# A Fourier mixing layer and a gated MLP on one core: half of each form's copies compared by accumulating DMAs, stored places reused later, loads spaced, h loaded from GpSimd's queue

## The chip, the cores and the metric

The kernel runs on one NeuronCore of a Trainium2 chip. Its engines work side by side and each takes its instructions in order: TensorE (PE; PEld for its weight loads) multiplies matrices, VectorE (DVE) and ScalarE (ACT) work elementwise, GpSimd (POOL) does small things and issues DMAs, SyncE (SP) issues DMAs only. A DMA's transfer is carried out by 16 DMA engines that all queues share. The metric is the device time of one execution in microseconds (us); lower is better.

## What is computed

```python
def reference(A_x, A_dft_seq_re, A_dft_seq_im, A_dft_hid_re, A_dft_hid_im, B_x, B_w1, B_w3, B_w2, gate_w):
    x = A_x                                           # 1 x 2048 x 512, float32
    g = sigmoid((x * gate_w).sum(-1, keepdims=True))
    a = einsum("bsd,ed->bse", x, dft_hid_re)          # 512 x 512
    b = einsum("bsd,ed->bse", x, dft_hid_im)
    y = einsum("ts,bse->bte", dft_seq_re, a) - einsum("ts,bse->bte", dft_seq_im, b)   # 2048 x 2048
    h = silu(x @ w1) * (x @ w3)                       # 512 x 1376 each
    out = h @ w2                                      # 1376 x 512
    return g * y + (1 - g) * out
```

The float32 products are made as three products of float32r parts: each operand is split into a rounded part ("high", on ScalarE) and the remainder ("low", on VectorE).

## The kernel before

The work runs in stages, with TensorE going from one to the next.

**Gate phase** (up to about 205 us). For 22 items (a chunk c of 128 columns of w1 and w3, and a half of the rows of x) seven products give x·w1 and x·w3 in Strassen's manner, and silu(gate)·up goes to DRAM as `hs` (`store_h`, L298, GpSimd's queue). Weights come in as `ws` (L193) and, for the second pass over a chunk, as finished parts `wb` (L200), both on SP.

**H** (about 205 to 333 us). `HSTEPS` (L910) has 22 steps, 11 chunks for each of two halves of 1024 rows. A step m multiplies a chunk of h (`ht`) by a chunk of w2 into eight PSUM banks, three matmuls a bank, 24 in all. The chunk for step m+4 is loaded (`load_h`, L914, SP) and that for m+2 is split (`high_h`, `low_h`) during step m. In the last step of a half each bank j is scaled by 1 − g into a tile `nb` (L1042 on VectorE and L1047 on ScalarE in turn), and every second one a store of two banks to `nbsp` goes out (L1043, GpSimd's queue).

**O and E** (about 333 to 349 us). Instead of the full Fourier matrices the kernel uses their symmetries: x is folded into four forms, O1a, O1b, O2 and E2 (`make_forms`, L807; the split result is `xf`), and each is multiplied by one stored tile of the matrix (`mov`, from `rep`). The results go through `e`, `s` and `z` (L1099 on) and are split again.

**Y** (from there on). Ten units of 15 short matmuls (128 or 130 columns) multiply z by the hidden matrix `DT`; VectorE adds and subtracts (L1161), combines with g and the stored `nbsp` (L1175), and SP writes the output.

**The comparison.** The symmetries hold only if the given matrices are Fourier matrices. So every stored tile is compared with the 15 other places of the matrix that should be equal to it or its negative: `wt` holds 16 tiles of 128 x 1024 for each form, the first eight of one sign, the others of the other. `compare(kind, keep)` (L713) makes tasks: load `rep` and take the sum of its absolute values (`size_rep`); load a copy, subtract or add `rep` on VectorE (`differ`, L672), sum the absolute difference on ScalarE into a column of `acc` (`add_up`, L683). With `keep` the same `rep` also yields `mov`; without it `make_mov` (L727) loads `rep` once more. The small tables have comparisons of their own (`compare_d`, `compare_small`). `verdict` (L533) compares all columns with the sizes, and if it fails, the program goes on to a general computation (`tc.If`, L1192 on), which doesn't run here.

**The order of that work.** Tasks for ScalarE ("A") and VectorE ("D") wait in `QUEUE`. The main loops call `work(eng, us)` (L565) at fixed places: it emits as many ready tasks of that engine as fit the given cost. A task is ready when its load was issued at least `LAG` calls earlier and the tasks that it needs were issued in an earlier call. Every call ends with `load_ahead` (L553), which issues loads in order on SP while at most 26 loaded tasks are unissued and free places remain beyond `RES`. Places are 4 KB tiles in a list `F4`; `take` draws the first and `free` appends, both at the time of emission, so a place can be drawn while its last reader is still at work, and the drawer waits. The calls are: in the gate phase from item 9 on, three an item; in H, at j = 1, 3, 4 and 6 of a step (L1022 to 1035); then some in O, and two in each of the first eight units of Y. Before O, `work_until(0, n_first)` (L1050) emits what is left of the tasks up to the forms, the whole comparison of O1a and all `mov` tiles; at the ninth unit of Y, `work_until(0, n_late)` emits all the rest.

Of the kernel before, what the change touches and what calls it, by code (L numbers as in the profile page):

```python
# [30 lines left out]
def fnet_swiglu_gate_kernel(  # L31
# [497 lines left out]
    acc, rep_sum = tail[:, :80], tail[:, 80:96]  # L529
    g_raw, g_pos, g_neg = (tail[:, 96 + 16 * k : 112 + 16 * k] for k in range(3))  # L530
    flag = tail[:, 144:160]

    def verdict():  # L533


        v = acc.rearrange("p (g n) -> p g n", n=16)
        nc.vector.scalar_tensor_tensor(v, v, TOL, rep_sum[:, :5, None].to_broadcast([P, 5, 16]),
                                       op0=ALU.mult, op1=ALU.is_le)
        nc.vector.tensor_reduce(flag[:, :1], acc, axis=mybir.AxisListType.X, op=ALU.add)

    def verdict_end(ps):
        nc.tensor.matmul(ps[:1, :1], flag[:, :1], nc.const_aps.tensor(1.0, [P, 1], F32), start=True, stop=True)
        nc.vector.tensor_scalar(flag[:1, 2:3], ps[:1, :1], 80.0 * P, None, op0=ALU.is_lt)
# [8 lines left out]

    def load_ahead(n):  # L553
        for i in ORDER:
# [3 lines left out]
            if sum(k not in ISSUED for k in LOADED) >= n or len(F4) < need + temps + HELD_BACK[0] + RES[0]:  # L558
                return
            if f:  # L560
                f()
            HELD_BACK[0] += temps
            LOADED[i] = NOW[0] if f else -99

    def work(eng, us, most=9, lag=None):  # L565


        NOW[0] += 1
        lag = LAG[0] if lag is None else lag
        for i in ORDER[:LIMIT[0]]:  # L570
# [5 lines left out]
            if i not in LOADED or NOW[0] - LOADED[i] < lag or any(ISSUED.get(k, NOW[0]) >= NOW[0] for k in after):  # L576
# [10 lines left out]
    def work_until(lo, hi):  # L587
        for _ in range(200):
            if all(i in ISSUED for i in range(lo, hi)):
# [57 lines left out]
    def high_x(form):  # L647
        XF[form] = lp.tile([P, 2, 1024], F32R, tag=f"m1_{GROUPS.index(form)}", name=f"xf_{form}")
        high(XF[form][:, 0], XR[form])

    def low_x(form):
        src = XR.pop(form)
        low(XF[form][:, 0], XF[form][:, 1], src)
# [14 lines left out]
    def load_t(i, src):  # L668
        TR[i] = wide(f"t{i}")
        nc.sync.dma_start(TR[i][:, : src.shape[-1]], src)  # L670

    def differ(kind, i):  # L672
        t, r = TR[16 * GROUPS.index(kind) + i], REP[kind]
        if i < 8:
            nc.vector.tensor_sub(t, t, r)  # L675
        elif kind != "E2":
            nc.vector.tensor_add(t, t, r)  # L677
        else:
            tv, rv = halves(t), halves(r)
            nc.vector.tensor_sub(tv[:, :, 0], tv[:, :, 0], rv[:, :, 0])  # L680
            nc.vector.tensor_add(tv[:, :, 1], tv[:, :, 1], rv[:, :, 1])  # L681

    def add_up(i, n=1024):  # L683
        t = TR.pop(i)
        nc.scalar.activation(t[:, :n], t[:, :n], AF.Abs, accum_out=acc[:, i : i + 1])  # L685
# [15 lines left out]
    def low_mov(kind, held=REP):  # L701
# [3 lines left out]
        if kind == "E2":  # L705
            nc.gpsimd.memset(MV[kind][:, :, :, 257].bitcast(F32), 0.0)
            nc.gpsimd.memset(MV[kind][:, :, 1::2, 128].bitcast(F32), 0.0)
            for par in range(2):
                nc.gpsimd.tensor_scalar(MV[kind][:, :, 2 * par, 128], MV[kind][:, :, 2 * par, 0].bitcast(F32),
                                        1.0 - 2.0 * par, None, op0=ALU.mult)  # L710


    def compare(kind, keep):  # L713
# [3 lines left out]
        users = task("A", 1.2, lambda: size_rep(g, REP[kind]), (), lambda: load_rep(kind), 1, 1),  # L717
        if keep:
            h = task("A", 1.0, lambda: high_mov(kind), (*users, -1))
            users += task("D", 1.2, lambda: low_mov(kind), (h,)),  # L720
        for i in range(1, 16):
            d = task("D", 1.4 if kind == "E2" and i > 7 else 1.2, lambda i=i: differ(kind, i), (),
                     lambda i=i: load_t(16 * g + i, wt[16 * g + i]), 1)
            task("A", 1.2, lambda i=i: add_up(16 * g + i), (d,))
        task("D", 0.0, lambda: free(REP.pop(kind)), (*users, d))

    def make_mov(kind):  # L727
        h = task("A", 1.0, lambda: high_mov(kind, ONCE), (-1,), lambda: load_rep(kind, ONCE), 1)
        task("D", 1.2, lambda: low_mov(kind, ONCE), (h,))
# [7 lines left out]
    def differ_d(i):  # L737
        t, r = TR[64 + i], DH[0]
# [680 lines left out]
```

## Time and profile before

| | us |
|---|---|
| median of 3 runs | 400.15 (399.53 to 402.89) |
| the profiled execution | 400.1 |
| its span, first to last instruction | 398.0 |

| stage, us from the span's start | PE busy | DVE | ACT | DMA share | granted clock |
|---|---|---|---|---|---|
| 100 to 140 (gate phase) | 40.00 | 32.34 | 27.28 | 0.71 | 1.00 |
| 140 to 200 (gate phase) | 57.63 | 48.03 | 31.83 | 0.98 | 1.00 |
| 205 to 333 (H) | 121.49 | 104.15 | 77.51 | 0.83 | 0.99 |
| 333 to 349 (O, E) | 15.62 | 7.66 | 5.03 | 0.95 | 1.00 |
| 355 to 390 (Y) | 34.57 | 33.26 | 21.27 | 0.58 | 0.50 |

The profile is of one execution. A row "A <- B" among the waits says that engine A was idle before the instruction named until B finished; "out<-in" names the tiles that an instruction writes and reads. In the last four columns of a stretch's row stand GpSimd's busy time, the TensorE clock that was granted (1.00 is full speed), the share of time in which the 16 DMA engines were busy, and GB/s.

### The profile page before, as it was taken

Reading aid. Unit: us, or ns where it says so; the run is one execution under the profiler, and the core shown is the slowest. Engines: PE = TensorE matmul, PEld = TensorE weight load, DVE = VectorE, ACT = ScalarE, POOL = GpSimd, SP = SyncE. Lnnn points to the kernel's source line nnn. Section 1 sums busy time; section 2 is a strip of 40 time slices with the busy share of each in tenths; the row PEclk is TensorE's granted clock in tenths of the full one; section 3 lists DMA queues with packets and bytes.
Section 4 is the critical chain, followed back from the end, with each engine's and each line's share of the span. In section 5 each row is a group of like instructions: output and inputs, shape, how many; then the busy total and the mean of one; then the engine's idle time right before and its main releaser. Section 6 shows DMA issues by size and latency. Waiting matters only on the chain.

```text
span 398.0 us, 5255 instructions
## 1 busy us (share of the span) xinstructions
PE 375.5 (94%) x1750; PEld 324.7 (82%) x1750; DVE 324.9 (82%) x464; ACT 234.1 (59%) x399; POOL 52.6 (13%) x105
## 2 busy tenths in 40 slices
PE   9999999999999989999998999994999999959992
PEld 5888888888888868888787888883888889849992
DVE  4999899997788959888768788886869779189992
ACT  5867765565567748543445366242859767179440
POOL 0001122111111111111114713002000002000000
PEclk9999999999999999999999999998999999975555
DMA  7459766673278999999976699694599999975651
GB/s 294 180 214 368 266 226 249 237 291 133 82 237 280 409 404 324 342 333 416 264 301 182 215 413 378 235 310 160 196 366 415 417 410 396 362 215 178 233 184 58
DMA packets 34786, 111.18 MB, mean 279 GB/s; under 512 B 5954, under 2 KB 6211, under 8 KB 32708
## 3 DMA queue, kind: packets, MB, share of 16 engines
q1 hardware_dynamic: 28868, 86.68, 60.7%
q0 software_dynamic: 5888, 24.13, 15.1%
q8 instruction: 15, 0.25, 0.2%
q14 instruction: 15, 0.12, 0.1%
HBM read 82.48 MB, written 28.32 MB: 278 GB/s over the span
## 4 chain that ended last, share of the span: by engine, by line
PE 64%; DVE 12%; DMA 11%; issue 5%; ACT 4%; POOL 1%; SPq 0%; ACTq 0%; DVEq 0%; POOLq 0%
PE X L125 22%; PE H L125 12%; PE Z L125 10%; PE Y L125 6%; DMA nbsp<-nb 3%; DMA tail<-gs 3%; DMA ws<-w 3%; PE C L125 3%; DMA w2r<-w 3%; DVE ht L114 2%; DVE t L675 2%; DVE w2t L114 1%; PE wps L384 1%; DVE nb L1042 1%; ACT t L685 1%
## 5 line engine op out<-in xcount | busy, mean ns | idle before, releaser
L125 PE MATMUL H<-w2t,ht 128*128 128x512 f32 (+1 forms) x528 | 117.0, 384 | 6.5 <-ACT nb L1047 5.2
L125 PEld LDWEIGHTS H<-w2t,ht 128*128 128x128 f32 (+1 forms) x528 | 100.5, 191 | 23.1 <-ACT nb L1047 6.4
L125 PE MATMUL X<-xo,wb 128*128 128x512 f32 x378 | 89.1, 380 | 2.4 <-DMA wb<-wbsp 1.6
L685 ACT ACTIVATE t<-t 128x1024 f32<-128x1024 f32 (+1 forms) x68 | 67.6, 1000 | 26.0 <-DVE t L681 10.0
L125 PEld LDWEIGHTS X<-xo,wb 128*128 128x128 f32 x378 | 71.2, 189 | 13.6 <-DMA wb<-wbsp 2.0
L298 POOL DMA_DIRECT2D hs<-h x40 | 21.8, 544 | 115.9 <-DVE h L358 83.3
L114 DVE TENSOR_TENSOR ht<-hr,ht 128x1024 fp32r<-128x1024 f32 x22 | 28.2, 1280 | 10.6 <-ACT ht L111 10.5
L675 DVE TENSOR_TENSOR t<-t,rep 128x1024 f32<-128x1024 f32 x28 | 33.3, 1217 | 0.0
L125 PE MATMUL Z<-xo,wb 128*128 128x512 f32 x126 | 30.6, 379 | 0.0
L125 PE MATMUL Z<-xo,wa 128*128 128x512 f32 x126 | 30.6, 379 | 0.0
L125 PE MATMUL X<-xo,wa 128*128 128x512 f32 x126 | 30.6, 379 | 0.0
L125 PE MATMUL Y<-xo,wa 128*128 128x512 f32 x126 | 30.6, 379 | 0.0
L111 ACT ACTIVATE ht<-hr 128x1024 fp32r<-128x1024 f32 x22 | 23.1, 1050 | 12.2 <-DMA hr<-hs 10.8
L677 DVE TENSOR_TENSOR t<-t,rep 128x1024 f32<-128x1024 f32 x24 | 28.1, 1220 | 0.0
L125 PEld LDWEIGHTS X<-xo,wa 128*128 128x128 f32 x126 | 23.8, 189 | 3.4
L125 PEld LDWEIGHTS Y<-xo,wa 128*128 128x128 f32 x126 | 23.8, 189 | 3.4
L125 PEld LDWEIGHTS Z<-xo,wb 128*128 128x128 f32 x126 | 23.8, 189 | 3.4
L125 PEld LDWEIGHTS Z<-xo,wa 128*128 128x128 f32 x126 | 23.8, 189 | 3.4
L114 DVE TENSOR_TENSOR wa<-ws,wa 128x768 fp32r<-128x768 f32 (+1 forms) x22 | 19.3, 881 | 7.7 <-ACT wa L111 7.5
L111 ACT ACTIVATE wa<-ws 128x768 fp32r<-128x768 f32 (+2 forms) x21 | 17.0, 808 | 13.4 <-DMA ws<-w 8.9
L369 ACT ACTIVATE h<-X 128x512 f32<-128x512 f32 x20 | 11.9, 595 | 21.6 <-PE X L125 21.5
L349 DVE TENSOR_TENSOR u<-u,X 128x512 f32<-128x512 f32 x21 | 14.4, 686 | 11.1 <-PE X L125 9.0
(292 smaller groups left out, 536.2 us busy)
## 6 DMA issues: line engine op xcount, KB each, us to landing
t<-wt SPq DMA_DIRECT2D x60, 512.0 KB, 7.9
hr<-hs SPq DMA_DIRECT2D x22, 512.0 KB, 7.3
hs<-h POOLq DMA_DIRECT2D x40, 256.0 KB, 4.3
wbsp<-wb POOLq DMA_DIRECT2D x8, 1024.0 KB, 4.2
wb<-wbsp SPq DMA_DIRECT2D x8, 1024.0 KB, 9.7
ws<-w SPq DMA_DIRECT2D x11, 512.0 KB, 4.9
xs_B<-xt SPq DMA_DIRECT2D x8, 512.0 KB, 5.5
xr<-xw SPq DMA_DIRECT2D x8, 512.0 KB, 8.5
```

The source lines that it names most:

```text
L111: nc.scalar.activation(hi, src, AF.Copy)
L114: nc.vector.tensor_sub(lo, src, hi.bitcast(F32))
L125: nc.tensor.matmul(ps.rearrange("p (n a) -> p n a", a=2), u, turns(v)[:, some], **kw)
L298: nc.gpsimd.dma_start(hs[c][:, b * TB : (b + 1) * TB], h)
L349: nc.vector.tensor_add(u4, u4, x)
L369: nc.scalar.activation(g1, x, AF.Silu)
L384: nc.tensor.matmul(wps, warm[:, :P], warm, start=True, stop=True)
L675: nc.vector.tensor_sub(t, t, r)
L677: nc.vector.tensor_add(t, t, r)
L685: nc.scalar.activation(t[:, :n], t[:, :n], AF.Abs, accum_out=acc[:, i : i + 1])
L1042: nc.vector.tensor_scalar(to, H[j], by, None, op0=ALU.mult)
```

## The change

For O1a, O1b and O2, the eight copies of equal sign are loaded as before. From seven of them `rep` is subtracted into a second tile `a` (`apart`), which is summed. Onto each loaded copy itself, and for the last one onto `rep`, a copy of the other sign is then added by an accumulating DMA on GpSimd's queue (`opposite`), and ScalarE sums the absolute value of what is left. For E2 the tiles are laid out anew on the host (real parts first, then imaginary parts): the imaginary halves of the other sign are accumulated (`opposite_im`, 256 KB each), and four tiles with the remaining real halves have `rep`'s real half subtracted (`apart_re`). A form thus has up to 20 columns in `acc` instead of 16.

A sum that follows an accumulating DMA is marked `(d, True)`, and `passed` lets it be emitted only `LAND` calls after the task that issued the DMA (4 in the gate phase, 8 from H on). `free_later` gives the place of a stored `nb` back after `LAND` calls, not at once. `load_ahead` has tokens: `RATE` of them (0.8, from H on 0.6) come with each call, at most 1.5 are held, a load spends one for each tile and waits while the count is below zero. `RES` is 5 in the last three steps of a half and 2 otherwise. The loads of h from m = 6 on are issued on GpSimd's queue. O1b and E2 are compared with `keep`, so `rep` is loaded once for each; the tasks that must be emitted before O are now a set, `MUST` (forms, edges, `mov` tiles, `DT`), and the rest of O1a's comparison is not among them. `xf` takes two places of `F4` for each form; the pool that it lived in becomes eight further places from the gate phase on. In H's second half every other step has one more `work("A", 1.2)`.

```diff
+    def free_later(*tiles):
+        for t in tiles:
+            _, places, at = HELD.pop(id(t))
+            COLD.append((NOW[0] + LAND[0], places, at))
+
+    def thaw():
+        for c in [c for c in COLD if c[0] <= NOW[0]]:
+            COLD.remove(c)
+            c[1].append(c[2])
+
+    def passed(k):
+        k, wait = k if isinstance(k, tuple) else (k, False)
+        return k in ISSUED and ISSUED[k] + (LAND[0] if wait else 1) <= NOW[0]
+
     def load_ahead(n):
+        thaw()
         for i in ORDER:
...
+            if f and TOKENS[0] < 0:
+                return
             if f:
                 f()
+                TOKENS[0] -= need
...
+        TOKENS[0] = min(TOKENS[0] + RATE[0], 1.5)
...
-    def work_until(lo, hi):
+    def work_until(ids):
+        ORDER.sort(key=lambda i: i not in ids)
...
     def high_x(form):
-        XF[form] = lp.tile([P, 2, 1024], F32R, tag=f"m1_{GROUPS.index(form)}", name=f"xf_{form}")
-        high(XF[form][:, 0], XR[form])
+        XF[form] = [take(F4, [P, 1024], F32R, f"xf{h}_{form}") for h in range(2)]
+        high(XF[form][0], XR[form])
...
-    def differ(kind, i):
-        t, r = TR[16 * GROUPS.index(kind) + i], REP[kind]
-        if i < 8:
-            nc.vector.tensor_sub(t, t, r)
-        elif kind != "E2":
-            nc.vector.tensor_add(t, t, r)
-        else:
-            tv, rv = halves(t), halves(r)
-            nc.vector.tensor_sub(tv[:, :, 0], tv[:, :, 0], rv[:, :, 0])
-            nc.vector.tensor_add(tv[:, :, 1], tv[:, :, 1], rv[:, :, 1])
+    def apart(g, i):
+
+        t = TR[20 * g + i] = wide(f"a{g}_{i}")
+        nc.vector.tensor_sub(t, TR["up", g, i], REP[GROUPS[g]])
+
+    def opposite(g, i):
+
+        nc.gpsimd.dma_start(TR["up", g, i], wt[16 * g + 8 + i], accum_op=ALU.add)
+        TR[20 * g + 8 + i] = TR.pop(("up", g, i))
+
+    def opposite_im(g, i):
+        t = TR["up", g, i]
+        nc.gpsimd.dma_start(t[:, 512:], wt[16 * g + 12 + i // 2][:, 512 * (i % 2) : 512 * (i % 2) + 512],
+                            accum_op=ALU.add)
+        TR[20 * g + 12 + i] = TR.pop(("up", g, i))
+
+    def apart_re(g, j):
+        t, r = TR[20 * g + 8 + j], REP[GROUPS[g]]
+        tv = t.rearrange("p (k n) -> p k n", k=2)
+        nc.vector.tensor_sub(tv, tv, r[:, None, :512].to_broadcast([P, 2, 512]))
...
-        for i in range(1, 16):
-            d = task("D", 1.4 if kind == "E2" and i > 7 else 1.2, lambda i=i: differ(kind, i), (),
-                     lambda i=i: load_t(16 * g + i, wt[16 * g + i]), 1)
-            task("A", 1.2, lambda i=i: add_up(16 * g + i), (d,))
-        task("D", 0.0, lambda: free(REP.pop(kind)), (*users, d))
+        def sum_of(i, d):
+            if kind == "E2":
+                task("A", 0.7, lambda: add_up(20 * g + 12 + i, 1024, 512), ((d, True),))
+            else:
+                task("A", 1.1, lambda: add_up(20 * g + 8 + i), ((d, True),))
+
+        def part(i):
+            apart(g, i)
+            meet(i)
+
+        for i in range(1, 8):
+            d = task("D", 1.2, lambda i=i: part(i), (), lambda i=i: load_t(("up", g, i), wt[16 * g + i]), 1, 1)
+            task("A", 1.1, lambda i=i: add_up(20 * g + i), (d,))
+            sum_of(i, d)
+            users += d,
+        if kind == "E2":
+            for j in range(4):
+                d = task("D", 1.2, lambda j=j: apart_re(g, j), (),
+                         lambda j=j: load_t(20 * g + 8 + j, wt[16 * g + 8 + j]), 1)
+                task("A", 1.1, lambda j=j: add_up(20 * g + 8 + j), (d,))
+                users += d,
+
+        def last():
+            TR["up", g, 0] = REP.pop(kind)
+            meet(0)
+
+        d = task("D", 0.0, last, users)
+        sum_of(0, d)
...
     compare("O1a", True)
+    MUST.update(range(n_forms))
     make_mov("O2")
     make_d()
-    make_mov("O1b")
-    make_mov("E2")
-    n_first = len(QUEUE)
+    compare("O1b", True)
+    compare("E2", True)
     compare_small()
-    compare("O1b", False)
-    compare("E2", False)
...
-            nc.sync.dma_start(HR[m], hs[c][:, half * 1024 : (half + 1) * 1024])
+            (nc.sync if m < 6 else nc.gpsimd).dma_start(HR[m], hs[c][:, half * 1024 : (half + 1) * 1024])
...
-            F4.extend((lp, f"f4_{k}") for k in range(8, 14))
+            F4.extend((lp, f"f4_{k}") for k in range(8, 22))
...
-    LAG[0], RES[0] = 4, 2
+    LAG[0], LAND[0], RATE[0] = 4, 8, 0.6
...
+        RES[0] = 5 if i > NC - 4 else 2
...
             if j == 6:
                 work("D", 1.3)
+                if half and m % 2 and not last:
+                    work("A", 1.2)
...
-                    free(nbt)
+                    free_later(nbt)
...
-    work_until(0, n_first)
+    work_until(MUST)
```

More of the change, by code (lines that the diff above doesn't have):

```diff
@@ L528, in fnet_swiglu_gate_kernel @@
     tail = const.tile([P, 160], F32, tag="tail", name="tail")
-    acc, rep_sum = tail[:, :80], tail[:, 80:96]
-    g_raw, g_pos, g_neg = (tail[:, 96 + 16 * k : 112 + 16 * k] for k in range(3))
-    flag = tail[:, 144:160]
+    acc, rep_sum = tail[:, :100], tail[:, 100:108]
+    g_raw, g_pos, g_neg = (tail[:, 108 + 16 * k : 124 + 16 * k] for k in range(3))
+    flag = tail[:, 156:160]
     def verdict():
-        v = acc.rearrange("p (g n) -> p g n", n=16)
-        nc.vector.scalar_tensor_tensor(v, v, TOL, rep_sum[:, :5, None].to_broadcast([P, 5, 16]),
+        v = acc.rearrange("p (g n) -> p g n", n=20)
+        nc.vector.scalar_tensor_tensor(v, v, TOL, rep_sum[:, :5, None].to_broadcast([P, 5, 20]),
                                        op0=ALU.mult, op1=ALU.is_le)
@@ L575, in work @@
                 break
-            if i not in LOADED or NOW[0] - LOADED[i] < lag or any(ISSUED.get(k, NOW[0]) >= NOW[0] for k in after):
+            if i not in LOADED or NOW[0] - LOADED[i] < lag or not all(passed(k) for k in after):
                 continue
@@ L585, in fnet_swiglu_gate_kernel @@
     AHEAD = [26]
-    def work_until(lo, hi):
+    def work_until(ids):
+        ORDER.sort(key=lambda i: i not in ids)
         for _ in range(200):
-            if all(i in ISSUED for i in range(lo, hi)):
+            if all(i in ISSUED for i in ids):
                 return
@@ L989, in fnet_swiglu_gate_kernel @@
     f4d_cm, f4d = pool("f4d", 1, "right")
-    F4.extend((f4d, f"f4_{k}") for k in range(16, 23))
+    F4.extend((f4d, f"f4_{k}") for k in range(24, 31))
     w2_cm, w2p = pool("w2", 1, "right")
@@ L1182, in fnet_swiglu_gate_kernel @@
         if u == 8:
-            work_until(0, n_late)
+            work_until(set(range(n_late)))
             verdict()
```

65 lines of the change are left out of this document (41 added, 24 removed).

## The prediction, made before the change was run

> **What bounds the kernel now.** The page comes first, then who waited for whom, then the chain of waits, then stretches with their granted clock.
>
> ```profile
> span 398.0 us, 5255 instructions
> ...
> PE 375.5 (94%) x1750; PEld 324.7 (82%) x1750; DVE 324.9 (82%) x464; ACT 234.1 (59%) x399; POOL 52.6 (13%) x105
> ...
> PEclk9999999999999999999999999998999999975555
> DMA  7459766673278999999976699694599999975651
> ```
>
> TensorE is busy 94% of the span, so the kernel gets shorter only where TensorE waits, where its clock is low, or where another engine ends last. The clock row shows the second: in the last four or five slices of 10 us it is at or near half. TensorE's own waits are few (columns: total us, times, longest):
>
> ```profile
> PE H L125 <- ACT nb L1047: 5.2, 3, 3.4
> PE Y0a L125 <- ACT z_O L111: 2.7, 1, 2.7
> PE X L125 <- DMA wb<-wbsp: 1.6, 1, 1.6
> PE Y0a L125 <- ACT e L1100: 1.6, 1, 1.6
> ```
>
> The releaser is mostly ScalarE. What held ScalarE itself from 270 to 346 us:
>
> ```profile
> ACT nb L1047 <- DMA nbsp<-nb: 7.8, 2, 4.3
> ```
>
> The chain (start us, us, what) has the same stores, between the halves of H,
>
> ```profile
> 276.08 3.21 DMA nbsp<-nb
> ```
>
> and after H:
>
> ```profile
> 336.83 0.77 DVE nb L1042
> ...
> 338.99 6.20 DMA nbsp<-nb
> ...
> 345.30 0.61 ACT e L1100
> ```
>
> Each time the next step is held by the store of an evacuated bank: the place was given back when the store was issued, and the next nb (between the halves) or e0 (after H) drew that very place and had to see the store land. From here on the chain is TensorE alone, without a gap to the last unit of Y:
>
> ```profile
> 355.43 1.30 PE Y0a L125 x4
> ```
>
> ```profile
> 371.06 1.28 PE Y4b L125 x6
> 372.34 2.30 PE Y5a L125 x9
> ```
>
> The clock follows from the waits (the number behind the five engines is the granted clock, then the DMA share and GB/s):
>
> ```profile
> 275.00:276.00 1.00, 0.66 (x2) 0.57 (x3) 1.00 (x3) 0.87 (x2) 0.00 (x0) 0.76 0.00 0
> 276.00:277.00 1.00, 1.00 (x3) 0.80 (x3) 1.00 (x2) 0.00 (x0) 0.92 (x2) 0.50 0.00 0
> 278.00:279.00 1.00, 1.00 (x4) 0.82 (x3) 0.00 (x0) 0.00 (x0) 0.00 (x0) 0.53 0.86 315
> 370.00:375.00 5.00, 5.00 (x23) 4.64 (x23) 5.00 (x12) 1.43 (x3) 0.00 (x0) 0.50 0.53 183
> ```
>
> Behind the long wait between the halves it is half for 0.48 + 2 + 0.94 = 3.4 us, then full again. In Y it stays at 0.50 though TensorE is never without work.
>
> **The change, part by part.** The profiled execution took 400.1 us, 2.1 of it outside the span; the median is 400.15, so the sum is made against 400.1.
>
> *Places of stored banks reused later; five places kept back in the last three steps of a half.* This answers the waits between the halves.
>
> ```profile
> L125 PE MATMUL H<-w2t,ht 128*128 128x512 f32 (+1 forms) x528 | 117.0, 384 | 6.5 <-ACT nb L1047 5.2
> ```
>
> Matmuls of H follow one another every 117.0 / 528 = 0.222 us, so in its last step TensorE finishes a bank every 0.66 us; two engines evacuate in turn, 0.7 to 0.8 us each, so the evacuation keeps up and only the landing of the store (3.2) made it late. The 5.2 us go, and with them the half clock, which lost half of 3.4: **−6.9**. Late next is the evacuation, which keeps up: nothing.
>
> *The same after H.* TensorE goes on with O and E meanwhile and ends them here:
>
> ```profile
> 345.95 0.94 PE L125 MATMUL E_1a<-mov_E,xf_E 128*128 128x258 f32 x6 [0.38 <-ACT e L1100]
> ```
>
> ```profile
> 348.87 0.49 PE L125 MATMUL E_1b<-er_p,edge_p 1*1 1x258 f32 x3
> ```
>
> that is at 349.4, or 349.0 without its wait of 0.38. From e0 (345.3) the rest of z took until Y0a (355.43), 10.1 us. Begun when VectorE's last evacuation ends, at 337.6, it is done by 347.7, before TensorE needs it. So Y begins at 349.0 instead of 355.43; five of Y0a's nine matmuls had been done by then, at 0.21 (Y4b's 1.28 / 6) 1.1 us: 6.4 − 1.1 = **−5.3**.
>
> *Loads spaced by tokens.* This thins the bursts in the gate phase and may remove the 1.6 us that TensorE waits for wb. Bounds: 0 and −1.6; the row names a load that a burst explains, so **−1.6**.
>
> *Half of the copies by accumulating DMAs.* VectorE's part of it now:
>
> ```profile
> L677 DVE TENSOR_TENSOR t<-t,rep 128x1024 f32<-128x1024 f32 x24 | 28.1, 1220 | 0.0
> ```
>
> ```profile
> L681 DVE TENSOR_TENSOR t<-t,rep 128x512 f32<-128x512 f32 x8 | 5.6, 702 | 0.0
> L680 DVE TENSOR_TENSOR t<-t,rep 128x512 f32<-128x512 f32 x8 | 5.6, 702 | 0.0
> ```
>
> The 24 additions go, and for E2's eight pairs (11.2) come four subtractions at 1.22: 28.1 + 11.2 − 4.9 = 34.4 us less. VectorE's tasks from H on, counted in the code, fall from 66 to 46. This is off the path while TensorE leads, and counts in Y only if TensorE is faster there than VectorE (below). ScalarE sums as much as before (8 halves for 4 wholes); two repeated loads of rep fall away. The price:
>
> ```profile
> q0 software_dynamic: 5888, 24.13, 15.1%
> ```
>
> ```profile
> 205.00:333.00 128.00, 121.49 (x550) 104.38 (x550) 104.15 (x118) 77.51 (x128) 21.63 (x46) 0.99 0.83 308
> ```
>
> ```profile
> t<-wt SPq DMA_DIRECT2D x60, 512.0 KB, 7.9
> ```
>
> No accumulate is in the trace. GpSimd's queue moved 24.13 MB in 15.1% of 398 us of the 16 engines, 401 GB/s, so 512 KB take 1.31 us of all of them. The low end is that an accumulate costs what the load costs that it replaces (it brings the same bytes from the same place, so no gain); the high end is two more passes, one to read the destination and one for a write that waits for it, 2.6 us. H has 8 + 8 + half of 8 = 20 of them: 0 to 52 us of DMA time, 26 with one pass. H leaves 17% of 128 us free, 21.8, and the two reps give back 2.6: 24.4, about one pass. The nearest row is the load; I take it with part of one pass and charge nothing to the path. Landing: a sum on ScalarE is placed eight calls of work behind its accumulate, two steps of 24 matmuls, 10.7 us, against 7.9 for a load.
>
> The Trainium skill ("DMA: Bandwidth & Descriptors", Rules for kernel authors) says that an accumulating DMA reads its destination and writes it later. No run here shows it yet; an estimate from it, three movements for two, gives half a pass more, 13 us in H, still inside the cover.
>
> *Who waits behind it.* On GpSimd's queue the accumulate waits for its subtraction on VectorE; behind it stand the loads of h from the seventh on, the bank stores and the small copies of the forms. A load of h is issued almost two steps before ScalarE splits it: 0 while VectorE is less than that late, one step (5.3) each time it isn't.
>
> *h on GpSimd's queue* lifts it over comparison loads that wait for places on SP:
>
> ```profile
> SPq L918 <- ACT t L685: 15.9, 3, 10.4
> ```
>
> TensorE's largest waits name no hr, so 0.
>
> *E2's banks in another order, xf in tile places, a verdict over 100 columns* only change addresses and small widths: 0.
>
> *Y.* A unit takes TensorE 2.30 + 1.28 = 3.58 us at half clock. VectorE beside it:
>
> ```profile
> 371.65 0.77 DVE L1161 TENSOR_TENSOR w<-Y3a,w 128x258 f32<-128x258 f32 x2
> 372.32 1.68 DVE L1175 SCALAR_TENSOR_TENSOR r<-w,tail,nbr 128x256 f32<-128x256 f32 x4
> 373.90 0.70 DVE L680 TENSOR_TENSOR t<-t,rep 128x512 f32<-128x512 f32 x1
> 374.50 0.70 DVE L681 TENSOR_TENSOR t<-t,rep 128x512 f32<-128x512 f32 x1
> ```
>
> ```profile
> 382.00 0.79 DVE L1161 TENSOR_TENSOR w<-Y6a,w 128x258 f32<-128x258 f32 x2
> 382.67 0.90 DVE L1175 SCALAR_TENSOR_TENSOR r<-w,tail,nbr 128x256 f32<-128x256 f32 x2
> ```
>
> The first four rows follow each other at once, 3.45 us from one L1161 to the next, all but equal to TensorE; without comparison work it is 2.45, and 1.69 in the last four units. While the clock is half this relief is worth nothing: ten units keep 35.8 us. But Y now begins at full clock, and one period of 3.4 us at full rate before it falls is **−1.7**.
>
> Sum: −6.9 − 5.3 − 1.6 − 1.7 = −15.5, so 384.6, said as **385**.
>
> **The rivals.** *The clock holds through Y.* VectorE then sets the pace: 6 × 2.45 + 4 × 1.69 = 21.5, with 2.5 for the first unit's way to VectorE 24 instead of 35.8: 11.8 less, 1.7 of it counted already, so 384.6 − 10.1 = 374.5, **374**. For it: waits of 1.6 us left the clock full, and only the longest ones (3.4, 2.7) brought it down. Against it: 30 us of Y without a gap did not raise it, so these short matmuls weigh little, and at VectorE's pace there are fewer of them in a microsecond of TensorE's time at full clock.
>
> The Trainium skill ("TensorE: Matmul & The Clock Gate", Part 1) has full clock after one busy window of about 3.4 us and half after an idle one. The 3.4 us between the halves agree; Y, busy for 30 us at 0.50, does not. By that rule a Y that begins at full clock and never idles for a window keeps it, which is this rival.
>
> *The work reappears in Y.* Spaced loads and two places for each copy make E2's comparison late; VectorE takes two subtractions with a unit (2.4), 2.45 + 2.4 = 4.9 over TensorE's 3.58. If all 12 of E2's tasks are left, six units lose 1.3 each, 8 us, and the last accumulate with its sum (7.9 and 1) stands before the verdict; 8 + 6 or so of 15.5 are given back, **399**. For it: the pairs L680 and L681 ran there before. Against it: 20 tasks fewer.
>
> *Slower: accumulates saturate the DMA engines in H.* H's DMA time is 0.83 × 128 = 106, less 2.6, plus 26 for each extra pass. At one pass it is 129.6, about as long as H is now: the point from which it decides. At one and a half it is 142.6; h lands late behind accumulates on its own queue, ScalarE stands in order before sums that have not landed, and H takes 14.6 longer than its 128. With the 6.9 inside H swallowed and 8.6 kept, 400.1 + 14.6 − 8.6 = **406**; at two passes 419. For it: the DMA row has nines through much of H. Against it: late copies can slide into Y, where the DMA share is 0.53.
>
> **How the numbers follow.** Chances: forecast (385, own range 379 to 391) 0.40; held clock (374, 369 to 379) 0.24; work in Y (399, 394 to 404) 0.14; saturated (406, 402 to 420) 0.22. With both signs in it the range runs from 370, nearly the bottom of the held clock, to 405, which takes in one pass and leaves out most of the saturated case: some 0.03 below, 0.16 above. One per cent, 4 us, is about what a measurement can tell. Faster than 396.1: 0.40 + 0.24 = 0.64; within 1%: nearly all of the third case, 0.13; slower: the saturated one and a rest of the third, 0.23.
>
> **What would show it.** Right: no wait for nbsp on ScalarE, clock 1.00 between the halves, Y0a directly behind E_1b, units of 3.58 with the clock falling soon after Y begins, VectorE with idle time there. Held clock: units of about 2.5 and no fives in the clock row. Work in Y: subtractions of copies beside the units. Saturated: accumulates landing later than 11 us, ScalarE waiting for them and for hr, a DMA share near 1 through H. The forecast is wrong if TensorE's waits in H add up to more than 6 us.

## The result, and the profile after

The changed kernel takes 432.98 us, the median of four runs (430.88 to 435.57), beside 400.2 for the kernel before on the same chip: a ratio of 1.081, 95% interval 1.073 to 1.089. The forecast was 385, the range 370 to 405; the direction was wrong. The profiled execution took 430.9 us.

These lines are from the page of the changed kernel. In the rows of queues stand packets, MB and the share of 16 engines' span; in those of instructions, busy us, mean ns of one, and the idle time before them with what ended most of it.

```profile
span 429.0 us, 5216 instructions
...
PE 384.9 (90%) x1750; PEld 326.7 (76%) x1750; DVE 291.8 (68%) x428; ACT 234.6 (55%) x407; POOL 91.4 (21%) x153
...
PEclk9999999999999969989999999998966998899655
DMA  8469665635287999999897344589998999999761
...
q0 software_dynamic: 12800, 47.20, 37.3%
...
L125 PE MATMUL H<-w2t,ht 128*128 128x512 f32 (+1 forms) x528 | 128.7, 406 | 22.0 <-ACT ht L111 13.4
...
L111 ACT ACTIVATE ht<-hr 128x1024 fp32r<-128x1024 f32 x22 | 23.1, 1048 | 43.1 <-DMA hr<-hs 40.9
...
L703 POOL DMA_DIRECT2D up<-wt x21 | 18.1, 864 | 53.8 <-DVE a L699 26.7
```

VectorE fell from 324.9 to 291.8 us, 33.1, as the change meant it to (34.4 was predicted), and the span rose by 31.0. TensorE is busy 90% instead of 94%. The DMA row has nines from about 140 to 225 us and eights and nines from 280 to about 395, with a hollow (threes to fives) between them. H's matmuls were idle for 22.0 us, most of it for ScalarE's split of h, and ScalarE in turn stood 40.9 us for the landing of h. More than 6 us of waits in H was the forecast's own sign of being wrong. TensorE's own list of waits (total, times, longest) names the two stages that lost:

```profile
PE H L125 <- ACT ht L111: 13.4, 4, 5.8
PE X L125 <- DMA wb<-wbsp: 8.9, 2, 4.6
PE X L125 <- DVE u L349: 3.5, 3, 1.8
```

The store of nb is gone from the top of the list. The chain of waits of the changed kernel shows transfers in its place, one in the gate phase and three in H, the two longest of which stand here, and behind them Y:

```profile
143.21 22.43 DMA xr<-xw
...
314.13 9.88 DMA hr<-hs
...
357.64 10.02 DMA hr<-hs
...
391.69 1.43 PE Y0a L125 x9
...
398.98 0.72 PE Y3b L125 x6
399.70 2.31 PE Y4a L125 x9
```

Stages are best bounded by the first matmul of H and the first of O, here in the timeline of the changed kernel:

```profile
226.46 13.87 PE L125 MATMUL H<-w2t,ht 128*128 128x512 f32 x63 [1.44 <-ACT h L369]
...
376.21 0.60 PE L125 MATMUL O<-mov_O1a,xf_O1a 128*128 128x256 f32 x3 [0.52 <-ACT nb L1119]
```

The same two places read from the timelines of the kernel before and of the experiments below give this table (us):

| kernel | H begins | O begins | span | H | from O on |
|---|---|---|---|---|---|
| before | 211.0 | 333.3 | 398.0 | 122.3 | 64.7 |
| changed | 226.5 | 376.2 | 429.0 | 149.7 | 52.8 |
| before + places later (e4) | 210.7 | 327.5 | 385.8 | 116.8 | 58.3 |
| changed, second copies left out (e3) | 210.3 | 331.3 | 387.3 | 121.0 | 56.0 |
| changed, second copies loaded plainly (e2) | 217.7 | 347.3 | 402.5 | 129.6 | 55.2 |
| the same, h on SP (f3) | 218.1 | 339.8 | 396.8 | 121.7 | 57.0 |
| accumulates in the gate phase only (f1) | 226.7 | 347.6 | 404.6 | 121.0 | 57.0 |
| accumulates after the gate phase only (f2) | 210.0 | 360.7 | 417.7 | 150.7 | 57.0 |

The gate phase lost 15.5 us and H 27.4; from O on 11.9 were gained: 15.5 + 27.4 − 11.9 = 31.0, the difference of the spans. (The stage table ahead of the forecast starts H at 205 us; its first matmul is at 211.0.) The stretches of the changed kernel show what the DMA engines did meanwhile (the last three columns are the granted clock, the DMA share and GB/s):

```profile
140.00:200.00 60.00, 48.12 (x200) 40.13 (x199) 33.17 (x42) 30.11 (x54) 9.07 (x14) 0.91 1.04 354
...
220.00:275.00 55.00, 51.65 (x236) 44.05 (x235) 40.89 (x51) 27.36 (x42) 22.46 (x44) 1.00 0.56 191
275.00:371.00 96.00, 77.38 (x297) 62.15 (x297) 44.76 (x46) 49.38 (x83) 25.21 (x34) 0.88 0.96 273
```

In the gate phase and in the larger part of H the engines are full, and H's first part leaves 44% of 55 us, 24 us of them, unused.

TensorE's losses make up these sums. In H it waited 22.0 us instead of 6.5 and its matmuls took 128.7 instead of 117.0: 15.5 + 11.7 = 27.2 of the 27.4. The second term agrees with the clock: 0.88 over 96 us is worth an estimated 0.12 × 96 = 11.5 us. In the gate phase the waits for wb and u rose from 1.6 and 0.5 to 8.9 and 3.5, and the clock of 0.91 over 60 us adds an estimated 5.4: 15.7 of 15.5. In Y the clock works the other way: the first four units took 8.0 us at full clock instead of 4 × 3.58 = 14.3. With the 5.3 of the earlier start that is 11.6 of the 11.9.

### The profile page after: what moved, and what is told of

It is laid out like the page before. It is cut to its first block, busy times and chain, and to the rows that moved or that the text cites. A ratio compares the mean times of both kernels' runs of the same rounds, so it can differ in the third digit from the quotient of the medians.

```text
span 429.0 us, 5216 instructions
## 1 busy us (share of the span) xinstructions
PE 384.9 (90%) x1750; PEld 326.7 (76%) x1750; DVE 291.8 (68%) x428; ACT 234.6 (55%) x407; POOL 91.4 (21%) x153
## 3 DMA queue, kind: packets, MB, share of 16 engines
q0 software_dynamic: 12800, 47.20, 37.3%
## 4 chain that ended last, share of the span: by engine, by line
PE 42%; issue 28%; DMA 12%; POOL 9%; ACT 3%; DVE 3%; SPq 0%; POOLq 0%; ACTq 0%; DVEq 0%
PE X L125 17%; PE Z L125 8%; DMA hr<-hs 6%; DMA xr<-xw 5%; PE Y L125 5%; PE C L125 3%; PE O L125 2%; POOL up L703 2%; POOL hs L298 2%; ACT ht L111 1%; POOL edge L860 1%; DMA xs_B<-xt 1%; POOL hr L987 1%; ACT a L719 1%; POOL rep L703 1%
## 5 line engine op out<-in xcount | busy, mean ns | idle before, releaser
L125 PE MATMUL H<-w2t,ht 128*128 128x512 f32 (+1 forms) x528 | 128.7, 406 | 22.0 <-ACT ht L111 13.4
L125 PEld LDWEIGHTS H<-w2t,ht 128*128 128x128 f32 (+1 forms) x528 | 105.9, 203 | 44.7 <-ACT ht L111 15.5
L125 PE MATMUL X<-xo,wb 128*128 128x512 f32 x378 | 92.2, 389 | 12.5 <-DMA wb<-wbsp 8.9
L125 PEld LDWEIGHTS X<-xo,wb 128*128 128x128 f32 x378 | 72.5, 193 | 25.3 <-DMA wb<-wbsp 9.7
L114 DVE TENSOR_TENSOR ht<-hr,ht 128x1024 fp32r<-128x1024 f32 x22 | 27.9, 1269 | 53.1 <-ACT ht L111 53.1
L111 ACT ACTIVATE ht<-hr 128x1024 fp32r<-128x1024 f32 x22 | 23.1, 1048 | 43.1 <-DMA hr<-hs 40.9
L699 DVE TENSOR_TENSOR a<-up,rep 128x1024 f32<-128x1024 f32 x28 | 33.2, 1217 | 2.6 <-DMA up<-wt 2.6
L719 ACT ACTIVATE a<-a 128x1024 f32<-128x1024 f32 x28 | 29.3, 1046 | 6.5 <-DVE a L699 6.5
L125 PE MATMUL Z<-xo,wb 128*128 128x512 f32 x126 | 32.3, 395 | 0.0
L703 POOL DMA_DIRECT2D up<-wt x21 | 18.1, 864 | 53.8 <-DVE a L699 26.7
L719 ACT ACTIVATE up<-up 128x1024 f32<-128x1024 f32 (+1 forms) x28 | 26.3, 939 | 4.1 <-DMA up<-wt 4.1
L369 ACT ACTIVATE h<-X 128x512 f32<-128x512 f32 x20 | 11.9, 594 | 29.9 <-PE X L125 25.2
L125 PEld LDWEIGHTS Z<-xo,wb 128*128 128x128 f32 x126 | 25.1, 199 | 4.0
L349 DVE TENSOR_TENSOR u<-u,X 128x512 f32<-128x512 f32 x21 | 14.4, 684 | 20.3 <-PE X L125 15.5
```

The lines of the kernel that those rows point to most:

```text
L111: nc.scalar.activation(hi, src, AF.Copy)
L114: nc.vector.tensor_sub(lo, src, hi.bitcast(F32))
L125: nc.tensor.matmul(ps.rearrange("p (n a) -> p n a", a=2), u, turns(v)[:, some], **kw)
L349: nc.vector.tensor_add(u4, u4, x)
L369: nc.scalar.activation(g1, x, AF.Silu)
L699: nc.vector.tensor_sub(t, TR["up", g, i], REP[GROUPS[g]])
```

## The experiments

Times are medians; ratios are to the kernel before on the same chip, with 95% intervals. A difference between two experiments is taken from their ratios, times 400.15 us. Every run that leaves out a part of the comparison (e2, e3, f1, f2, f3, g1, g4, p1) also has the verdict's factor `TOL` set to 0, so that the short path is taken.

**e1: h back on SP.**

```diff
-            (nc.sync if m < 6 else nc.gpsimd).dma_start(HR[m], hs[c][:, half * 1024 : (half + 1) * 1024])
+            nc.sync.dma_start(HR[m], hs[c][:, half * 1024 : (half + 1) * 1024])
```

> The changed kernel with one part undone: all loads of h are issued on SP's queue again. Three theories. Engine time (an accumulate of 512 KB takes the 16 DMA engines about 2.8 us instead of 1.31, so they are full at 140 to 200 and 275 to 380 us and everything lands late): no byte changes, so 424 to 436. Queue order (h stands on GpSimd's queue behind accumulates, stores and their waits): TensorE's 13 to 22 us of waiting in H go, about 410. Spacing (tokens and the eight more places put the loads of x and of the copies at a bad time, whatever they are): no change, 430.

Measured: 427.46, 1.0662 [1.0638, 1.0686]. The queue accounts for 0.0147, 5.9 us; most of the loss stays when h no longer stands behind the accumulates.

**e2: plain loads in the place of the accumulating DMAs.**

```diff
-nc.gpsimd.dma_start(TR["up", g, i], wt[16 * g + 8 + i], accum_op=ALU.add)
+nc.gpsimd.dma_start(TR["up", g, i], wt[16 * g + 8 + i])
```

and the same for `opposite_im`.

> The changed kernel with the accumulating DMAs made plain loads of the same bytes into the same tiles from the same queue: copies of the other sign overwrite instead of being added, so the second half of the comparison is left out, and the verdict's factor is 0 so that the short path is taken. Engine time: the DMA time falls by 28 x 1.5 = 42 us, and the time to 395 to 402. Queue order: GpSimd's queue holds the same instructions with the same waits, so 420 to 433. Spacing: 425 to 433.

Measured: 404.51, 1.0113 [1.0078, 1.0148], a little above what the theory of engine time gave and far below what the rivals gave. The same bytes on the same queue in the same order cost 27.9 us less when nothing is added. From the page of e2, its queue and its issuing instruction:

```profile
q0 software_dynamic: 12288, 47.20, 30.5%
```

```profile
L703 POOL DMA_DIRECT2D up<-wt x21 | 11.2, 533 | 38.0 <-DVE a L699 30.5 <-ACT mov_O1b L111 3.5 <-ACT rep L718 1.0
```

**e3: the accumulating DMAs left out.**

```diff
-nc.gpsimd.dma_start(TR["up", g, i], wt[16 * g + 8 + i], accum_op=ALU.add)
```

and the same for `opposite_im`.

> The changed kernel without the accumulating DMAs (24 of 512 KB and 8 of 256 KB left out; ScalarE sums the loaded copies as they are; factor of the verdict 0). It shows what all the rest of the change is worth. Engine time: 385 to 392, where the prediction was without a price for the accumulates. Queue order: the same 385 to 392, since nothing stands before h. Spacing: 420 or more, and TensorE still waits at 150 to 180 us.

Measured: 389.07, 0.969 [0.9631, 0.975], as expected. Everything else in the change together, without the second copies, is a gain; the second copies, 28 transfers' worth of 512 KB, cost 0.1119, 44.8 us. From the page of e3:

```profile
q0 software_dynamic: 8192, 32.52, 21.9%
```

The three queue rows give the price of a transfer. GpSimd's queue took 21.9% of 387.3 = 84.8 us of all 16 engines without second copies, 30.5% of 402.5 = 122.8 with plain ones, 37.3% of 429.0 = 160.0 with accumulating ones. For the 28 × 512 KB (47.20 − 32.52 = 14.68 MB) that is 38.0 / 28 = 1.36 us for a load and 75.2 / 28 = **2.69 us for an accumulate**: twice, one whole pass more. (This puts the whole difference of the queue's time down to the 28; f1 with 8 and f2 with 20 of them, below, give 2.65 and 2.76.) It shows in the stretch of e2 that answers to the changed kernel's last:

```profile
275.00:347.00 72.00, 63.84 (x277) 53.60 (x275) 40.99 (x39) 50.34 (x86) 18.68 (x37) 0.95 0.94 361
```

At nearly the same share, 0.94 and 0.96, all transfers together move 361 GB/s with plain loads and 273 with accumulates among them.

**e4: the kernel before, with only the places reused later and kept back.**

```diff
+            COLD.append((NOW[0] + 8, places, at))
...
+        RES[0] = 5 if i > NC - 4 else 2
...
-                    free(nbt)
+                    free_later(nbt)
```

> The kernel before with one part of the change alone: places of stored banks are given back eight calls later, and five places are kept back in the last three steps of a half. If the prediction's two terms hold (-6.9 between the halves, -5.3 before Y), 388; if another wait takes the place of the one removed, 396 to 401.

Measured: 387.72, 0.9655 [0.9625, 0.9685], as the two terms gave. It is the lowest median of the study, ahead of the kernels before and after; e3's interval overlaps it. Its page and TensorE's first wait in H:

```profile
PE 371.0 (96%) x1750; PEld 322.0 (83%) x1750; DVE 324.6 (84%) x464; ACT 233.2 (60%) x399; POOL 53.4 (14%) x105
...
PEclk9999999999999999999999999999999999995555
```

```profile
PE H L125 <- ACT nb L1058: 1.2, 1, 1.2
```

TensorE is busy 96%, and the dent in the clock between the halves is gone. e3, with 33 us less of VectorE's work, isn't faster than this. But e3 also has h on GpSimd's queue, which by itself costs e4 5.7 us (h1, below), and the new order, so it doesn't show what VectorE's relief alone is worth.

**f1 and f2: accumulates only for O2 (in the gate phase), and only for the other three forms.**

```diff
-        nc.gpsimd.dma_start(TR["up", g, i], wt[16 * g + 8 + i], accum_op=ALU.add)
+        if g == 2:
+            nc.gpsimd.dma_start(TR["up", g, i], wt[16 * g + 8 + i], accum_op=ALU.add)
```

with `opposite_im`'s left out as well; f2 has `g != 2` and keeps `opposite_im`'s.

> The changed kernel with accumulating DMAs for O2 alone (8, all in the gate phase); those of O1a, O1b and E2 are left out (24 and 8 minus 8, the sums take the loaded copies as they are; verdict's factor 0). Without any it took 389.1, with all 433. Engine time: 8 x 2.7 = 21.6 us more DMA time at 140 to 200 us, where the DMA engines are full, so the gate phase's stalls come back, 10 to 16 us: 399 to 405. Queue order (the harm comes in H, by h behind accumulates): 389 to 392.

> The counterpart: accumulating DMAs for O1a, O1b and E2, none for O2 (its 8 left out, verdict's factor 0). If the two parts add up, 389 + 44 less what the run with O2 alone costs, 415 to 425 by engine time; by queue order nearly all of it, 428 to 433.

Measured: f1 406.4, 1.0151 [1.0105, 1.0198], 18.4 us over e3, a little above its range; f2 418.48, 1.0452 [1.0389, 1.0515], 30.5 over e3, inside it. The two add up to 48.9, near the 44.8 of all together. In the table above f1 begins H as late as the changed kernel and has the H of e3; f2 has it the other way round. The stretches from 140 to 200 us of f1 and of f2, in this order, show the same:

```profile
140.00:200.00 60.00, 48.77 (x200) 40.49 (x199) 33.05 (x43) 29.98 (x54) 9.09 (x14) 0.89 1.04 354
```

```profile
140.00:200.00 60.00, 59.50 (x275) 51.44 (x273) 47.50 (x65) 36.65 (x70) 7.61 (x14) 1.00 1.00 366
```

Eight accumulates in the gate phase take 11 us of TensorE's work out of that stretch of 60 us, and in f2 it is untouched.

**g1: every second copy half as wide** (the second half of every comparison's columns is not added).

```diff
-nc.gpsimd.dma_start(TR["up", g, i], wt[16 * g + 8 + i], accum_op=ALU.add)
+nc.gpsimd.dma_start(TR["up", g, i][:, :512], wt[16 * g + 8 + i][:, :512], accum_op=ALU.add)
```

> The changed kernel with every accumulating DMA at half its width (256 KB instead of 512, 128 KB for E2; the other halves left out, verdict's factor 0): the same instructions, waits and places, half the bytes. Engine time: DMA time falls by half of 75 us, and the time about as with plain loads of full width, which take half the engine time too, 398 to 406. Queue order: the instructions and what they wait for are as before, 422 to 433.

Measured: 410.33, 1.0247 [1.018, 1.0314]. With as many instructions and waits on GpSimd's queue as in the changed kernel, half the bytes cost half the time (22.3 of 44.8 us over e3). That is above the 398 to 406 of engine time and far below the 422 to 433 of queue order, which is refuted. Its queue row:

```profile
q0 software_dynamic: 12800, 39.86, 31.5%
```

Of its span of 405.0 that is 127.6, 42.8 over e3, so the price holds, 1.53 us for 256 KB.

Set side by side, the extra time of the DMA engines over e3 and what it cost (us):

| | extra DMA time | cost over e3 | hidden |
|---|---|---|---|
| f1, gate phase alone | 21.2 | 18.4 | 2.8 |
| e2, plain | 38.0 | 16.9 | 21.1 |
| g1, half width | 42.8 | 22.3 | 20.5 |
| f2, after the gate phase | 55.1 | 30.5 | 24.6 |
| changed | 75.2 | 44.8 | 30.4 |

(f1: 26.2% of 404.6; f2: 33.5% of 417.7, less 84.8 each. All costs share e3's interval, ± 2.4.) In the four rows with transfers in H 20 to 30 us are hidden, though the extra time is 38 in one and 75 in another; what lies above is paid. In the gate phase nearly nothing is hidden.

**f3: plain loads, and h on SP**: e1's edit and e2's together.

> Plain loads in place of the accumulating DMAs (the second half of the comparison left out, verdict's factor 0), and h loaded on SP's queue. With h on GpSimd's queue this took 404.5. If h behind those loads is what is left of the harm (4.2 us of TensorE waiting for h in that trace), 398 to 400; if it is the DMA time of the loads at full stretches, 403 to 406; if h behind comparison loads on SP is worse, 406 to 410.

Measured: 396.59, 0.9904 [0.9873, 0.9936], below all three expectations. h on GpSimd's queue costs 0.0209, 8.4 us, with plain loads. In the table above it is all in H: 129.6 beside 121.7.

**h1: e4 with h on GpSimd's queue**, without any second copy there.

```diff
-            nc.sync.dma_start(HR[m], hs[c][:, half * 1024 : (half + 1) * 1024])
+            (nc.sync if m < 6 else nc.gpsimd).dma_start(HR[m], hs[c][:, half * 1024 : (half + 1) * 1024])
```

> The kernel before with places reused later (387.7 alone) and, added, the loads of h from the seventh on on GpSimd's queue; no accumulates. If that move costs by itself (it took 5.5 with accumulates and 8 with plain loads in front of it), 393 to 396; if it costs only behind other loads on that queue, 386 to 390.

Measured: 392.54, 0.9797 [0.9764, 0.983], 5.7 us over e4, nearly what the move was expected to cost by itself. The waits of h1 (e4 has 13.4 in the first row):

```profile
ACT ht L111 <- DMA hr<-hs: 20.6, 4, 10.2
POOL hr L928 <- ACT t L695: 11.3, 3, 6.1
POOL hr L928 <- DMA nbsp<-nb: 4.4, 1, 4.4
```

On GpSimd a load of h meets waits that have nothing to do with accumulates: it stands for the place that ScalarE's sum gives back, and for the landing of a store of nb.

**f4: no tokens.**

```diff
-            if f and TOKENS[0] < 0:
-                return
```

> The changed kernel with the tokens off: loads go out as soon as a place and the window of 26 tasks allow it, accumulates as changed. If the spacing is what makes the loads late and bunched (H's first half has a DMA share near 0.5, its second near 1), 415 to 425; if engine time of the accumulates sets it and the tokens hardly bind, 430 to 436; if the spacing helps as its name says, 437 or more.

Measured: 430.16, 1.074 [1.0669, 1.0812]. The interval overlaps the changed kernel's; spacing the loads gained nothing that shows, and TensorE waits for wb with tokens (8.9 us) as without (5.8).

**p1: f3 with the eight places of the new xf pool joining only when H begins.**

```diff
-F4.extend((lp, f"f4_{k}") for k in range(8, 22))
+F4.extend((lp, f"f4_{k}") for k in range(8, 14))
...
+    F4.extend((lp, f"f4_{k}") for k in range(14, 22))
```

> Plain loads in place of the accumulates, h on SP (second half of the comparison left out, verdict's factor 0; 396.6 in that form), and now the eight places that xf gave up join the list only when H begins. What is left there against 389 lies at 140 to 200 us: x's forms are loaded beside the second copies of O2. If the eight places cause that (more loads in flight at once), 389 to 391; if the second copies themselves do (they can start only behind the subtraction, so they fall into the full stretch), 395 to 398.

Measured: 397.44, 0.9875 [0.9822, 0.9929], not to be told from f3. More places are not what fills the gate phase's DMA engines.

**h2: e4 with the order of the change** (rep loaded once for O1b and E2, `MUST`), without accumulates.

```diff
-    make_mov("O1b")
-    make_mov("E2")
...
+    compare("O1b", True)
+    compare("E2", True)
```

> The kernel before with places reused later and with the order of the change that needs no accumulate: O1b and E2 compared with the kept rep (two loads of 512 KB fewer) and only forms, edges, mov tiles and the hidden matrix forced before O. TensorE waits little now, so 386 to 389 if Y at half clock (ten units of 3.58) ends last as before; below 385 only if VectorE's work in Y had been ending last.

Measured: 396.43, 0.9877 [0.9828, 0.9927]: the order by itself costs e4 8.9 us, where no loss was expected. The trace, of an execution that took 403.4 us, has this as TensorE's longest wait:

```profile
PE E_0a L125 <- POOL mov_E L720: 7.7, 1, 7.7
```

In the chain of that trace the split of mov_E stands on VectorE behind ten subtractions of the comparison, and GpSimd's work on it takes 4.85 us more. How much of it the other executions have isn't shown, so the cause stays open. In the changed kernel E follows O, and Y follows E, without a gap, so that it isn't a term of its time as it stands.

**g2, g3, g4, g5: the room for the descriptors of GpSimd's DMAs.** 512 instead of 1024 bytes a partition for the changed kernel (g2), for plain loads (g4) and for the kernel before (g5), and 1152 for the changed kernel (g3).

```diff
-    nc = bacc.Bacc("TRN2", target_bir_lowering=False, num_devices=1, dynamic_dma_scratch_size=1024)
+    nc = bacc.Bacc("TRN2", target_bir_lowering=False, num_devices=1, dynamic_dma_scratch_size=512)
```

> The changed kernel with half the memory set aside for the descriptors of GpSimd's DMAs (512 bytes a partition instead of 1024), all else as changed. GpSimd stood 20 us before accumulates with nothing named as the releaser. If it was waiting for room for descriptors, that idle time at least doubles and the time goes to 437 or more; if the accumulates' time on the DMA engines alone decides, 429 to 435 and the idle time stays near 20.

> The changed kernel with 1152 instead of 1024 bytes per partition for the descriptors of GpSimd's DMAs, nothing else changed. Halving the room cost 63 us (495.7 against 433.0). If the room already delays GpSimd's issues in the changed kernel (its page shows 19.4 us of issue idle before the accumulates), an eighth more should give some of it back: 422 to 430. If at 1024 the room is just enough and the engine time of the accumulates sets the end, nothing moves: 431 to 435.

> The plain-loads kernel (second half of every comparison overwritten, not added: that half is left out of the result) with 512 instead of 1024 bytes per partition for the descriptors. It moves the same bytes on GpSimd's queue as the changed kernel. If the room counts descriptors alone, it loses as much as the changed kernel did: 460 or more from 404.5. If what counts is how long the descriptors stay in it, and plain loads stay about half as long (1.36 against 2.69 us of engine time per 512 KB), it loses less than half as much: 406 to 430.

> The kernel before with 512 instead of 1024 bytes per partition for the descriptors. Its GpSimd queue moves 24.1 MB, the changed kernel's 47. If half the room binds any kernel, it is slower by 20 us or more; if the room binds only under the traffic that the change puts on GpSimd's queue, 399 to 404.

Measured: g2 495.74, 1.2371 [1.231, 1.2432]; g3 432.92, 1.0832 [1.0776, 1.0887]; g4 412.96, 1.0287 [1.0214, 1.0359]; g5 414.04, 1.0339 [1.0292, 1.0386]. Half the room costs the changed kernel 62.5 us, the plain loads 7.0 and the kernel before 13.6 (this last between its two expectations). An eighth more gives nothing back; a larger room wasn't tried. The waits of GpSimd's instructions for nothing that the profile shows, from the changed kernel, g2 and g5 in this order:

```profile
POOL up L703 <- issue: 14.5, 7, 4.2
```

```profile
POOL up L703 <- issue: 68.4, 14, 8.3
```

```profile
POOL nbsp L1043 <- issue: 16.1, 4, 4.6
```

With half the room the issues themselves stall, of accumulates in g2 and of the stores of nb in g5 (1.7 us in the kernel before).

Summed over all second copies, GpSimd stood 23.2 us in this way in the changed kernel, 23.4 in g3, 17.6 in g1, 12.6 in e1 and 1.4 before the plain loads of e2. So GpSimd stalls before accumulates at the changed kernel's own room as well; what for isn't shown. The stall by itself doesn't explain the cost over e3: in g1 it falls by a quarter and the cost by half, in e1 it falls by nearly half and the cost by an eighth.

## Why the prediction was wrong, step by step

**The step that failed** is the price of the accumulating DMAs: "The nearest row is the load; I take it with part of one pass and charge nothing to the path." Three things were wrong with it.

The size: an accumulate takes 2.69 us of all 16 engines where a load takes 1.36, one whole pass more. The bounds (0 to 2 passes) held it, and 26 us for H's 20 is what the forecast itself gave for one pass; the value taken was too low. Yet by the forecast's own cover of 24.4 one pass would have cost 1.6 us, so that the size alone doesn't explain the loss. The Trainium skill ("DMA: Bandwidth & Descriptors", Rules for kernel authors) has an accumulate read its destination and write it later. The trace agrees with an extra movement; the estimate of three movements for two was too low, since the time doubled.

The stretch: the eight accumulates of O2 fall into the gate phase, whose share of 0.98 stood in the table of the kernel before, and the forecast summed only H's. There they have no cover: H begins 7.4 us later with plain second copies than with none, and 16.2 later with accumulating ones (210.3, 217.7, 226.5).

The cover: 24.4 us were counted as free in H, and 24 us are free in it after the change, but in its first part (share 0.56 up to 275 us), while the accumulates come in the rest (0.96). The first accumulate of H is issued at 279.4. A mean share over 128 us said nothing about when the free time lies.

**h on GpSimd's queue** was priced at 0 because TensorE's largest waits named no hr. ScalarE's list of the kernel before did:

```profile
ACT ht L111 <- DMA hr<-hs: 10.8, 5, 4.1
```

It costs 5.7 us on e4, 5.9 in the changed kernel and 8.4 with plain loads. The row against SP's queue that the forecast quoted (15.9 us behind places) was answered by waits of the same kind on GpSimd.

**Who waits behind the accumulate**: bounds of 0 or 5.3 for each load of h, 0 taken. ScalarE stood 40.9 us for h in the changed kernel, and TensorE 13.4 for ScalarE's split. With h on SP (e1) these fall to 15.3 and 8.9, and H from 149.7 to 141.5 (229.1 to 370.5). So the queue is 8.2 us of it, and the rest, 20.5 over e3's 121.0, stays when h isn't behind the accumulates.

**Places reused later, between the halves and after H** (−6.9 and −5.3) held, with the −1.7 for Y's first period: together 13.9, measured in e4 13.8 [12.6, 15.0]. In the traces H gains 5.5, as 2.1 us of waits for the evacuation stay where none was forecast, and the rest from O on gains 6.4. In the changed kernel, too, no wait for nbsp is left and Y0a follows E_1b at once.

**The tokens** (−1.6) failed: the wait for wb rose from 1.6 to 8.9 us, and taking the tokens away moved nothing that can be told. In e3, with tokens and without second copies, TensorE has no wait for wb; in f1, with the gate phase's accumulates alone, it has 9.3. So the accumulates brought the wait back.

**VectorE's relief** was right in size (33.1 of 34.4). Its worth was taken as nothing, which agrees with Y's last six units, each a period of TensorE at half clock without a gap; no run changes VectorE's work alone, so it isn't shown by itself.

**The rivals.** The held clock is refuted: units of 3.58 us (2.30 and 1.28) from the fifth on. But the four units before them are 6.3 us shorter together than at half clock, where the forecast had 1.7. The work reappearing in Y wasn't seen: from O on the changed kernel is 11.9 us shorter than the kernel before. The saturated DMA engines are what happened. The rival's price for H, 14.6 us at one and a half passes, came out as 27.4 at one pass, for h's queue (7.9 by e2 against f3, 8.2 by the changed kernel against e1) and the unused first part of H lie on top; and it left the gate phase out altogether. Its evidence, the nines in the DMA row and a point of decision at one pass, was on the table.

The way from 400.15 to 433, by ratios: places reused later −13.8; the rest of the order with plain second copies, h on SP, +10.0 (e4 to f3; 7.5 of it is H's later begin); h on GpSimd's queue +8.4; the adding itself +27.9. That is 32.5 of the 32.4 us lost. What else in the order makes up the 10.0 besides the later second copies in the gate phase stays open.

## What to carry to other kernels

An accumulating DMA of this kind (128 x 1024 float32, from DRAM onto a tile) takes work from VectorE only to give twice a load's time to the DMA engines: cost it as two transfers, and do so stage by stage, against the share of the stage in which it falls. Where TensorE is made to wait, look at the granted clock too: in H the longer matmuls cost 11.7 us beside 15.5 of waits. A mean share over a long stage is no cover; look at shorter stretches for where the free time lies. And a load that a compute engine waits for shouldn't be moved behind instructions with waits of their own on another queue, even when its wait isn't on TensorE's list.

## What the runs showed of the hardware that was not expected

An accumulating DMA costs 2.69 us of all 16 engines per 512 KB beside 1.36 for a plain one, and its issue occupies GpSimd for 864 ns beside 533. GpSimd's issues stall when the room for their descriptors is short, and accumulates stall far more than loads: half the room cost 62.5 us with them and 7.0 with plain loads of the same bytes. Bytes alone don't order the loss: the kernel before, with half of them on that queue, lost 13.6.

The clock in Y falls without any idle time before it: the first four units of the changed kernel ran at full clock, about 2.0 us each from 391.69 on, and at 399.70, without a gap, the units became 3.58 us long and stayed so. The Trainium skill ("TensorE: Matmul & The Clock Gate", Part 1) lowers the clock after an idle window; this trace doesn't agree, as it fell after 8 us of uninterrupted short matmuls and never rose in the 20 us that followed. How long Y holds the full clock differs (8.0 us here, about 4 in e3 and 3 in e4, whose second unit began after a gap of 0.24), and what decides it wasn't tried.
